# First batch rotated in tiles of later weights, its turns four slots apart, and weight conversion from slot -8 at 1.5 slots a block

## The chip, the cores and the metric

The kernel runs on one core of a Trainium2 chip. The metric is the device time of one execution in microseconds; the median over several runs is compared. TensorE multiplies, VectorE, ScalarE and GpSimd (POOL in the rows) do elementwise work, and SP issues the transfers.

## The reference, cut to what matters

Rotary attention for 4 batches of 8 heads, 576 positions and 64 columns, then two layers of two matrix products each, without a choice of experts: every token passes all of them.

```python
q_rot, k_rot = rotate(q), rotate(k)                    # (x1 c - x2 s, x1 s + x2 c), per position
scores = matmul(q_rot, k_rot.T) / sqrt(D)
attn = exp(scores - max); attn = attn / (sum(attn) + 1e-9)
x = (attn @ v) as 2304 tokens x 512
h = x @ w_in;  r = max(h, 0);  x = (s * r * r + b) @ w_out          # layer one, d_ff 2048
h = x @ w_in2; out = (h * sigmoid(1.702 h)) @ w_out2                # layer two
```

The weights arrive as 64-bit floats, the rest as 32-bit floats.

## The kernel before

**Stages.** Attention is cut into *slots*: one slot is one score tile of 128 query rows against 576 keys. A batch has 36 slots (four pairs of heads; first four tiles for each pair, then five for each), four batches have 144. Layer one and layer two follow in passes of 256 or 512 tokens; each pass walks the 16 *blocks* `f` of 128 hidden columns. Pass 0 of layer one needs 256 tokens of all heads, so its first matmul (tile `l`) can stand only some slots behind slot 15; from slot 22 on the kernel interleaves half steps of the passes with slots.

**Numbers in two parts.** Products are taken in two parts each (`hi`, `lo`), so a weight block is kept as four 128x512 pieces. `weight(layer, f, m)` makes half `m` of block `f`: `make_half` (L383) loads 512 KB of 64-bit words into a `stage` tile (L389 or L394), scales the high words on ScalarE (L398), joins the words to 32-bit floats on VectorE (a shift, L399, and two joins, L400 and L403), copies `hi` on ScalarE (L406) and subtracts on GpSimd (L407). Stage tiles come from the ring `xs` of four halves. Blocks in `HELD` stay in tiles `w0` to `w10`; the five others of layer one are spilled to DRAM (L430) and fetched again in each pass. `CONV = (-12, 1.0)` gives block `f` of layer one the slot -12 + f, so 0 to 15 fall in slots -12 to 3.

**Rotation.** For each batch, pair and side (key, query) `plan_rope` (L658) sets a load into tile `nat` (L186), two slots later two cross products into `rot` (L195), a product (L200) and a sum (L203), then two *turns* (L205): transposes on TensorE (L91), a copy on ScalarE (L216), a subtraction on VectorE (L217), both into `z`, and stores to DRAM (L223, L224). `nat` and `rot` have two buffers each, in the pool of attention. In batch 0 the pairs start at slots -16, -12, -8 and -4; the queries of pairs 0 and 1 (`RV = 2`) are rotated on VectorE, the six other tiles on GpSimd. The turns of pair p stand at slots -12 + 4p to -10 + 4p.

**A slot.** `fetch_pair` loads turned keys and queries again (L229, L239, L241) four slots ahead of a unit. `score_tile` (L281) multiplies (tile `s`), reduces on VectorE (L299) and takes the exponential on ScalarE (L308); `norm_tile` scales on GpSimd (L319); `turn_tile` transposes, and up to slot 19 (`SLO`) `rest_tile` forms the low part with TensorE and ScalarE. `weighted` multiplies by the values (tile `av`), and the result goes to DRAM as `xT` (L378), from where `prepare` (L479) loads it for a pass.

**Order.** `at(slot, fn, ...)` collects tasks, `ORDER` sorts those of one slot, and the loop at L779 issues them slot by slot with the slot as priority. The order of each engine's queue is fixed when the program is built, from these priorities and the builder's own costs; on the chip each queue runs in that order and waits for what it needs. A load waits on SP, in order, until its buffer is free.

Of the kernel before, what the change touches and what calls it, by code (L numbers as in the profile page):

```python
# [26 lines left out]
def kernel(  # L27
# [65 lines left out]
    def f32(ap):  # L93
        return ap.bitcast(F32)
# [28 lines left out]
    q_spill = dram.tile([B * NP, 128, 2 * S], F32, tag="qsp", name="qsp")  # L123
    v_spill = dram.tile([B * NP, 128, 4 * 5 * D], F16, tag="vsp", name="vsp")
    qd = {}
    kd = {}
# [44 lines left out]
    def v_spread(b, st):  # L171
# [9 lines left out]
        vsc[b] = sc  # L181

    def rope_load(b, p, which, st):
        nat = att.tile([128, RT, 2, HD], F32, tag="nat", name=f"nat{b}{p}{which}")
        src = (q, k)[which][b, 2 * p : 2 * p + 2]
        nc.sync.dma_start(  # L186
            nat.rearrange("a t e i -> a t (e i)"),
            src.rearrange("h (a t) d -> (h a) t d", t=RT),
        )
        st["nat"] = nat  # L190

    def rope_cross(b, p, which, st, eng):
        rot = att.tile([128, RT, 2, HD], F32, tag="rot", name=f"rot{b}{p}{which}")
        for e in range(2):
            eng.tensor_tensor(rot[:, :, e], st["nat"][:, :, 1 - e], tab[:, 2 - e], op=ALU.mult)  # L195
        st["rot"] = rot
# [186 lines left out]
    def make_half(t, w_in, w_out, f, m, nm):  # L383
        if late:
            raw = late["m2"].tile([128, 512], U64, tag="stage", name=f"stage{nm}{m}", bufs=3)
        else:
            raw = moe.tile([128, 512], U64, tag="xs", name=f"stage{nm}{m}", bufs=4)
        if m == 0:
            nc.sync.dma_start(  # L389
                raw.rearrange("p (c f) -> p c f", c=NCC),  # L390
                w_in[:, f * 128 : (f + 1) * 128].rearrange("(c p) f -> p c f", p=128),
            )
        else:
            nc.sync.dma_start(raw, w_out[f * 128 : (f + 1) * 128, :])  # L394
        words = raw.bitcast(U32).rearrange("p (n z) -> p n z", z=2)
        low, high = words[:, :, 0], words[:, :, 1]
        hi, lo = t[:, 0], t[:, 1]
        nc.scalar.activation(f32(high), f32(high), AF.Copy, scale=2.0**-112)  # L398
        nc.vector.tensor_scalar(low, low, 29, None, op0=ALU.logical_shift_right)  # L399
        nc.vector.scalar_tensor_tensor(  # L400
            low, high, 0x80000000, low, op0=ALU.bitwise_and, op1=ALU.bitwise_or
        )
        nc.vector.scalar_tensor_tensor(  # L403
            low, high, 3, low, op0=ALU.logical_shift_left, op1=ALU.bitwise_or
        )
        nc.scalar.copy(hi, f32(low))  # L406
        nc.gpsimd.tensor_tensor(lo, f32(low), f32(hi), op=ALU.subtract)  # L407

# [5 lines left out]
    def weight(layer, f, m):  # L414
# [8 lines left out]
        if f not in STREAMED[layer]:  # L423
            t = kept[layer][f][m]
        make_half(t, *W[layer], f, m, f"{layer}_{f}")
        if f in STREAMED[layer]:
# [31 lines left out]

    late = {}

    def x_tile(nm, z=0):
# [196 lines left out]
    def plan_rope(b, p, which, s, eng):  # L658
# [4 lines left out]
        at(s + 2, rope_add, b, p, which, st, eng)  # L663
        gap = 2 if b else 1
        for g in range(2):
            at(s + 4 + gap * g, rope_turn, b, p, which, g, st)

# [9 lines left out]
    R0 = 20  # L677
    CONV = (-12, 1.0)
    WPRI = 0
# [3 lines left out]
    SLO = 20  # L683
    RS, RL = 9, 16
    MOE_LATE = 500

# [6 lines left out]
    def target(s):  # L693
# [5 lines left out]
        return 0  # L699
    RV = 2  # L700
    slot = 0
# [31 lines left out]
    for b in range(B):  # L733
        plan_scales(b, bounds[b] - R0 if b else -LEAD + 1)
        for p in range(NP):
# [3 lines left out]
            for which in (1, 0):  # L739
                eng = nc.vector if b == 0 and p < RV and which == 0 else nc.gpsimd  # L740
                r = bounds[b - 1] + RS + 9 * p if b else -RL + 4 * p
                plan_rope(b, p, which, r + (1 - which), eng)
# [105 lines left out]
```

## Time and profile before

| what | us |
|---|---|
| median of 3 runs | 1307.54 (1304.89 to 1314.07) |
| the profiled execution | 1307.66 |
| its span | 1305.9 |
| TensorE busy with matmuls | 1119.6 (86%) |
| VectorE busy | 746.5 (57%) |
| ScalarE busy | 676.7 (52%) |
| GpSimd busy | 354.8 (27%) |

The shares are means over the whole span. In the page's 40 slices TensorE is busy less than 70% in each of the first six (up to 196 us) and 80% or more in all others but one; VectorE and GpSimd have most of their dense slices early. The engines must therefore be read by stretch.

### The profile page before, as it was taken

The page shows a single profiled execution, that of the slowest core. Times are in us where ns is not written, and L with a number is a line of the kernel's source. Part 1 is how long each engine was busy: PE and PEld are TensorE (multiplying, and loading weights), DVE is VectorE, ACT ScalarE, POOL GpSimd, SP SyncE. Part 2 cuts the span into 40 slices and gives each one's busy share as a digit, 9 for nine tenths or more (in the row PEclk, how much of TensorE's full clock was granted, in tenths as well). Part 3 has the DMA queues.
Part 4 walks back from the last instruction along what each step waited for, and adds up shares of the span by engine and source line. Part 5 has one row for each costly group of instructions (what it writes and reads, how often), then busy time and mean ns, then how long its engine had stood idle before and what let it go on. Part 6 is the DMA issues. An engine that isn't in the chain of part 4 may idle for free.

```text
span 1305.9 us, 21075 instructions
## 1 busy us (share of the span) xinstructions
PE 1119.6 (86%) x7432; PEld 991.4 (76%) x7432; DVE 746.5 (57%) x1652; ACT 676.7 (52%) x1483; POOL 354.8 (27%) x350
## 2 busy tenths in 40 slices
PE   0126568989989989999999996998999999999998
PEld 0024448988889888899889996876788888888887
DVE  7887735667657666757656657866633223232222
ACT  3347555666656666666656655665533223232232
POOL 5675743334324441444111112323100000000000
PEclk9998588999999999999999997999999999999999
DMA  7987765468756677665665528545303012021020
GB/s 241 307 272 243 243 173 149 139 196 252 224 155 211 197 230 228 191 212 169 187 195 172 166 73 289 166 148 170 117 17 113 1 49 81 17 74 24 17 81 17
DMA packets 131561, 202.50 MB, mean 155 GB/s; under 512 B 32512, under 2 KB 93440, under 8 KB 131456
## 3 DMA queue, kind: packets, MB, share of 16 engines
q1 hardware_dynamic: 131456, 201.15, 49.4%
q8 instruction: 59, 0.97, 0.3%
q14 instruction: 46, 0.38, 0.1%
HBM read 155.49 MB, written 45.61 MB: 154 GB/s over the span
## 4 chain that ended last, share of the span: by engine, by line
PE 56%; DMA 14%; DVE 9%; issue 8%; ACT 5%; POOL 4%; SPq 2%; DVEq 0%; POOLq 0%; ACTq 0%
PE acc L88 21%; PE l L88 21%; PE t L88 5%; PE s L88 4%; PE av L88 4%; DMA stage<-in_moe_w_in_dram 2%; DMA xT<-pt 2%; DVE P L299 2%; POOL w L407 2%; DMA xl<-xT 2%; DMA stage<-in_moe_w_out_dram 2%; DMA vr<-in_v_dram 1%; ACT P L308 1%; DVE stage L403 1%; DVE pt L342 1%
## 5 line engine op out<-in xcount | busy, mean ns | idle before, releaser
L88 PE MATMUL l<-xh,w 128*128 128x256 f32 (+1 forms) x1280 | 330.0, 331 | 11.9 <-ACT r L527 6.8
L88 PEld LDWEIGHTS l<-xh,w 128*128 128x128 f32 x1280 | 225.0, 191 | 36.0 <-ACT r L527 8.0
L88 PE MATMUL l<-xl,w 128*128 128x256 f32 (+1 forms) x640 | 211.8, 331 | 1.6 <-DVE xl L492 0.9
L319 POOL TENSOR_SCALAR P<-P,st 128x576 f32<-128x576 f32 x144 | 114.1, 793 | 345.3 <-DVE st L318 241.5
L88 PE MATMUL acc<-w,g 128*128 128x512 f32 x696 | 169.0, 392 | 4.9 <-ACT y L568 4.9
L308 ACT ACTIVATE P<-P,st 128x576 f32<-128x576 f32 x144 | 112.0, 778 | 101.8 <-DVE P L299 101.8
L532 DVE SCALAR_TENSOR_TENSOR r<-r,l 128x256 f32<-128x256 f32 x144 | 60.1, 417 | 180.2 <-ACT r L531 180.2
L88 PEld LDWEIGHTS acc<-w,g 128*128 128x128 f32 x696 | 131.1, 189 | 33.0 <-ACT y L568 5.8
L88 PE MATMUL t<-ident,P 128*128 128x128 f32 x720 | 111.7, 289 | 45.2 <-ACT pt L357 29.4
L531 ACT ACTIVATE r<-l 128x256 f32<-128x256 f32 x144 | 55.1, 383 | 178.9 <-PE l L88 178.8
L299 DVE TENSOR_SCALAR_CACHE_REDUCE P<-s 128x576 f32<-128x576 f32 x144 | 108.6, 754 | 62.9 <-PE s L88 57.4
L407 POOL TENSOR_TENSOR w<-stage,w 128x512 fp32r<-128x512 f32 x64 | 93.2, 1461 | 188.3 <-ACT w L406 146.2
L88 PEld LDWEIGHTS l<-xl,w 128*128 128x128 f32 x640 | 122.1, 191 | 13.3 <-DVE xl L492 2.0
L88 PEld LDWEIGHTS t<-ident,P 128*128 128x128 f32 x720 | 86.1, 148 | 58.7 <-issue 23.3
L88 PE MATMUL acc<-gh,w 128*128 128x256 f32 x616 | 129.4, 293 | 0.0
L88 PE MATMUL s<-k,qb 128*128 128x288 f32 x640 | 124.9, 324 | 3.9 <-DVE P L299 3.9
L342 DVE TENSOR_TENSOR pt<-t,pt 128x640 f16<-128x640 f32 x124 | 102.0, 822 | 28.3 <-ACT pt L340 27.6
L340 ACT CAST pt<-t 128x640 f16<-128x640 f32 x144 | 99.1, 688 | 21.2 <-PE t L88 19.4
L536 DVE TENSOR_TENSOR g<-r,g 128x256 fp32r<-128x256 f32 x160 | 71.0, 448 | 64.7 <-ACT g L535 64.7
L88 PEld LDWEIGHTS s<-k,qb 128*128 128x128 f32 x640 | 98.6, 204 | 12.2 <-issue 6.3
L529 ACT ACTIVATE r<-r,sb 128x256 f32<-128x256 f32 x144 | 86.1, 604 | 37.2 <-DVE r L528 36.7
L88 PEld LDWEIGHTS acc<-gh,w 128*128 128x128 f32 x616 | 102.6, 194 | 0.5 <-issue 0.4
(88 smaller groups left out, 1955.5 us busy)
## 6 DMA issues: line engine op xcount, KB each, us to landing
ws<-wd SPq DMA_DIRECT2D x96, 512.0 KB, 4.3
k<-ksp SPq DMA_DIRECT2D x32, 576.0 KB, 5.8
stage<-in_moe_w_in_dram SPq DMA_DIRECT2D x32, 512.0 KB, 5.0
stage<-in_moe_w_out_dram SPq DMA_DIRECT2D x32, 512.0 KB, 5.0
wd<-w SPq DMA_DIRECT2D x14, 512.0 KB, 5.0
ksp<-z SPq DMA_DIRECT2D x32, 160.0 KB, 5.0
qsp<-z SPq DMA_DIRECT2D x32, 160.0 KB, 4.4
vsp<-vz SPq DMA_DIRECT2D x16, 320.0 KB, 4.5
```

What stands on the lines that cost most here:

```text
L88: pin(nc.tensor.matmul(*args, **kw))
L299: nc.vector.tensor_scalar(pr.rearrange("p (n s) -> p n s", n=2), ps[:, :, :HS], -Q_SCALE, None, op0=ALU.mult, op1=ALU.min, accum_out=st[:, ...
L308: nc.scalar.activation(pr, pr, AF.Exp, bias=st[:, 0:1], scale=-1.0, accum_out=st[:, 1:2])
L319: nc.gpsimd.tensor_scalar(pr, pr, st[:, 2:3], 1.0, op0=ALU.mult, op1=ALU.mult)
L340: nc.scalar.copy(hi, pc)
L342: nc.vector.tensor_tensor(lo, pc, hi, op=ALU.subtract)
L403: nc.vector.scalar_tensor_tensor(low, high, 3, low, op0=ALU.logical_shift_left, op1=ALU.bitwise_or)
L407: nc.gpsimd.tensor_tensor(lo, f32(low), f32(hi), op=ALU.subtract)
L529: nc.scalar.activation(r, r, AF.Identity, bias=sb[:, 1:2], scale=sb[:, 0:1])
L531: nc.scalar.activation(r, ps[:, cols], AF.Tanh, scale=0.851)
L532: nc.vector.scalar_tensor_tensor(r, r, 1.0, ps[:, cols], op0=ALU.add, op1=ALU.mult)
L536: nc.vector.tensor_tensor(gl[:, cols], r, f32(gh[:, cols]), op=ALU.subtract)
```

## The change

Batch 0's rotation no longer uses `nat`. Each pair gets one tile with the tag of a later weight block, `w5` to `w8` (blocks 7, 9, 10 and 12): it holds query, key and the key's `rot`. All eight loads are issued at slots -16 to -12 (pair p at -16 + p), the rotations two slots behind, and the turns are set apart from them: key of pair p at -8 + 4p and -7 + 4p, query a slot later. `RV` is 3, so the queries of pairs 0 to 2 are rotated on VectorE, five tiles on GpSimd.

Conversion of layer one has `CONV = (-8, 1.5)`: block `f` at slot int(-8 + 1.5 f), 0 to 15 at slots -8 to 14. Blocks below 13 are staged in two tiles of the weights, `w10` for even and `w9` for odd blocks, each holding both halves of a block; blocks 13 to 15 use `xs` as before. In layer one the last two steps (copy of `hi`, subtraction) become a function `split` that is called a slot later (`WLAG`). `ACT_SHIFT` is empty, so the shift stays on VectorE.

```diff
--- before.py
+++ after.py
@@ -122,6 +122,8 @@
     k_spill = dram.tile([B * NP, 128, 2 * S], F32, tag="ksp", name="ksp")
     q_spill = dram.tile([B * NP, 128, 2 * S], F32, tag="qsp", name="qsp")
     v_spill = dram.tile([B * NP, 128, 4 * 5 * D], F16, tag="vsp", name="vsp")
+    boot = {}
+    BOOT = (5, 6, 7, 8)
     qd = {}
     kd = {}
     vsc = {}
@@ -180,8 +182,16 @@
         nc.vector.tensor_copy(inv[64:128, o : o + NP], pv[64:128, :, 1])
         vsc[b] = sc
 
+    def boot_part(p, i):
+        return boot[p][:, i * S : (i + 1) * S].rearrange("p (t e i) -> p t e i", t=RT, e=2)
+
     def rope_load(b, p, which, st):
-        nat = att.tile([128, RT, 2, HD], F32, tag="nat", name=f"nat{b}{p}{which}")
+        if b == 0:
+            if p not in boot:
+                boot[p] = wpool.tile([128, 2048], F32, tag=f"w{BOOT[p]}", name=f"boot{p}")
+            nat = boot_part(p, which)
+        else:
+            nat = att.tile([128, RT, 2, HD], F32, tag="nat", name=f"nat{b}{p}{which}")
         src = (q, k)[which][b, 2 * p : 2 * p + 2]
         nc.sync.dma_start(
             nat.rearrange("a t e i -> a t (e i)"),
@@ -190,7 +200,10 @@
         st["nat"] = nat
 
     def rope_cross(b, p, which, st, eng):
-        rot = att.tile([128, RT, 2, HD], F32, tag="rot", name=f"rot{b}{p}{which}")
+        if b == 0 and which == 1:
+            rot = boot_part(p, 2)
+        else:
+            rot = att.tile([128, RT, 2, HD], F32, tag="rot", name=f"rot{b}{p}{which}")
         for e in range(2):
             eng.tensor_tensor(rot[:, :, e], st["nat"][:, :, 1 - e], tab[:, 2 - e], op=ALU.mult)
         st["rot"] = rot
@@ -383,6 +396,12 @@
     def make_half(t, w_in, w_out, f, m, nm):
         if late:
             raw = late["m2"].tile([128, 512], U64, tag="stage", name=f"stage{nm}{m}", bufs=3)
+        elif f < HELD[0][-2]:
+            if m == 0:
+                stages[0] = wpool.tile(
+                    [128, 2, 512], U64, tag=f"w{len(HELD[0]) - 1 - f % 2}", name=f"stage{nm}"
+                )
+            raw = stages[0][:, m]
         else:
             raw = moe.tile([128, 512], U64, tag="xs", name=f"stage{nm}{m}", bufs=4)
         if m == 0:
@@ -396,15 +415,22 @@
         low, high = words[:, :, 0], words[:, :, 1]
         hi, lo = t[:, 0], t[:, 1]
         nc.scalar.activation(f32(high), f32(high), AF.Copy, scale=2.0**-112)
-        nc.vector.tensor_scalar(low, low, 29, None, op0=ALU.logical_shift_right)
+        if m in ACT_SHIFT and not late:
+            nc.scalar.activation(low, low, AF.Copy, scale=2.0**-29, bias=-0.5)
+        else:
+            nc.vector.tensor_scalar(low, low, 29, None, op0=ALU.logical_shift_right)
         nc.vector.scalar_tensor_tensor(
             low, high, 0x80000000, low, op0=ALU.bitwise_and, op1=ALU.bitwise_or
         )
         nc.vector.scalar_tensor_tensor(
             low, high, 3, low, op0=ALU.logical_shift_left, op1=ALU.bitwise_or
         )
-        nc.scalar.copy(hi, f32(low))
-        nc.gpsimd.tensor_tensor(lo, f32(low), f32(hi), op=ALU.subtract)
+
+        def split():
+            nc.scalar.copy(hi, f32(low))
+            nc.gpsimd.tensor_tensor(lo, f32(low), f32(hi), op=ALU.subtract)
+
+        return split
 
     W = ((w_in1, w_out1), (w_in2, w_out2))
     kept = ({}, {})
@@ -422,7 +448,11 @@
             kept[layer][f] = [t[:, 0:2], t[:, 2:4]]
         if f not in STREAMED[layer]:
             t = kept[layer][f][m]
-        make_half(t, *W[layer], f, m, f"{layer}_{f}")
+        split = make_half(t, *W[layer], f, m, f"{layer}_{f}")
+        if layer == 0:
+            at(int(CONV[0] + CONV[1] * f) + WLAG, split)
+        else:
+            split()
         if f in STREAMED[layer]:
             d = dram.tile([128, 2, 512], F32, tag=f"wd{layer}{f}{m}", name=f"wd{layer}{f}{m}")
             spill[layer][f, m] = d
@@ -457,6 +487,7 @@
             )
 
     late = {}
+    stages = {}
 
     def x_tile(nm, z=0):
         if late and z == 0:
@@ -661,9 +692,8 @@
         at(s + 2, rope_cross, b, p, which, st, eng)
         at(s + 2, rope_mul, b, p, which, st, eng)
         at(s + 2, rope_add, b, p, which, st, eng)
-        gap = 2 if b else 1
         for g in range(2):
-            at(s + 4 + gap * g, rope_turn, b, p, which, g, st)
+            at(s + 4 + 2 * g if b else 4 * p + RT0 - which + g, rope_turn, b, p, which, g, st)
 
     def plan_scales(b, s):
         st = {}
@@ -675,13 +705,16 @@
 
     LEAD = 12
     R0 = 20
-    CONV = (-12, 1.0)
+    CONV = (-8, 1.5)
     WPRI = 0
     LAG = 6
     SKEW_T = 2
     SPILL = 2
     SLO = 20
     RS, RL = 9, 16
+    RT0 = -7
+    ACT_SHIFT = ()
+    WLAG = 1
     MOE_LATE = 500
 
     def avail(n):
@@ -697,7 +730,7 @@
                 start = max(0, 2 * NF * n - SKEW)
                 return start + min(1.0, (s - lo) / (hi - lo)) * (2 * NF * (n + 1) - SKEW - start)
         return 0
-    RV = 2
+    RV = 3
     slot = 0
     starts = {}
     bounds = []
@@ -737,8 +770,8 @@
             for kk in range(2):
                 at(starts[b, p, kk] - 4, fetch_pair, b, p, kk)
             for which in (1, 0):
-                eng = nc.vector if b == 0 and p < RV and which == 0 else nc.gpsimd
-                r = bounds[b - 1] + RS + 9 * p if b else -RL + 4 * p
+                eng = nc.vector if b == 0 and (p < RV and which == 0) else nc.gpsimd
+                r = bounds[b - 1] + RS + 9 * p if b else -RL + p
                 plan_rope(b, p, which, r + (1 - which), eng)
             vt = {}
             at(first - 4, value_load, b, p, vt)
```

## Rows read from the trace of the kernel before

**Rows 1.** Timeline of TensorE, 190 to 196 us: start, length, instruction, wait.

```profile
194.63 0.58 PE L88 MATMUL l<-xh,w 128*128 128x256 f32 x1 [4.16 <-ACT xh L491]
```

**Rows 2.** Windows: length, then busy us (instructions) by engine, granted clock, DMA share, GB/s.

```profile
7.50:99.10 91.60, 18.73 (x66) 12.44 (x67) 82.24 (x113) 36.68 (x68) 64.40 (x50) 1.00 0.88 285
99.10:153.50 54.40, 32.04 (x172) 23.72 (x170) 46.19 (x83) 37.00 (x70) 38.49 (x31) 0.76 0.74 237
153.50:194.60 41.10, 26.20 (x173) 20.67 (x173) 14.60 (x52) 22.94 (x44) 16.60 (x21) 0.75 0.68 201
194.60:1305.90 1111.30, 1042.59 (x7022) 934.54 (x7022) 602.54 (x1399) 578.76 (x1302) 234.59 (x244) 0.98 0.45 139
```

**Rows 3.** Timeline of VectorE: score reductions of slots 0, 3, 14, 17, 21, 22.

```profile
70.93 0.76 DVE L299 TENSOR_SCALAR_CACHE_REDUCE P<-s 128x576 f32<-128x576 f32 x1 [0.40 <-PE s L88]
...
99.13 0.76 DVE L299 TENSOR_SCALAR_CACHE_REDUCE P<-s 128x576 f32<-128x576 f32 x1 [0.88 <-PE s L88]
...
158.79 0.76 DVE L299 TENSOR_SCALAR_CACHE_REDUCE P<-s 128x576 f32<-128x576 f32 x1 [2.16 <-PE s L88]
...
174.35 0.76 DVE L299 TENSOR_SCALAR_CACHE_REDUCE P<-s 128x576 f32<-128x576 f32 x1 [0.48 <-PE s L88]
...
187.27 0.76 DVE L299 TENSOR_SCALAR_CACHE_REDUCE P<-s 128x576 f32<-128x576 f32 x1 [0.37 <-PE s L88]
...
190.60 0.76 DVE L299 TENSOR_SCALAR_CACHE_REDUCE P<-s 128x576 f32<-128x576 f32 x1
```

**Rows 4.** Waits of TensorE, 0 to 200 us: total us, times, longest.

```profile
PE r L91 <- POOL nat L203: 47.2, 5, 12.9
```

**Rows 5.** Timeline, 7 to 21 us: rotation on GpSimd, conversion steps alone and colliding.

```profile
7.57 1.82 POOL L195 TENSOR_TENSOR rot<-nat,tab 128x288 f32<-128x288 f32 x2 [6.27 <-DMA nat<-in_k_dram]
...
9.47 1.50 POOL L200 TENSOR_TENSOR nat<-nat,tab 128x576 f32<-128x576 f32 x1
...
11.05 1.79 POOL L203 TENSOR_TENSOR nat<-nat,rot 128x576 f32<-128x576 f32 x1
...
13.72 0.68 DVE L400 SCALAR_TENSOR_TENSOR stage<-stage 128x512 uint32<-128x512 uint32 x1
14.32 0.41 DVE L399 TENSOR_SCALAR stage<-stage 128x512 uint32<-128x512 uint32 x1
...
18.73 1.30 POOL L407 TENSOR_TENSOR w<-stage,w 128x512 fp32r<-128x512 f32 x1 [1.33 <-ACT w L406]
18.81 1.76 DVE L400 SCALAR_TENSOR_TENSOR stage<-stage 128x512 uint32<-128x512 uint32 x1
```

**Rows 6.** Groups by line, VectorE then GpSimd, 0 to 153.5 us: busy, mean ns, idle.

```profile
L400 DVE SCALAR_TENSOR_TENSOR stage<-stage 128x512 uint32<-128x512 uint32 x32 | 34.3, 1071 | 5.7 <-ACT stage L398 4.9
...
L407 POOL TENSOR_TENSOR w<-stage,w 128x512 fp32r<-128x512 f32 x32 | 46.6, 1459 | 25.1 <-ACT w L406 24.9
...
L203 POOL TENSOR_TENSOR nat<-nat,rot 128x576 f32<-128x576 f32 x8 | 14.3, 1782 | 0.2
...
L319 POOL TENSOR_SCALAR P<-P,st 128x576 f32<-128x576 f32 x12 | 11.7, 976 | 16.1 <-DVE st L318 8.4 <-ACT stage L398 3.1 <-DMA vr<-in_v_dram 2.3
```

**Rows 7.** Timeline, 36 to 41 us: a query tile rotated on VectorE.

```profile
36.25 0.81 DVE L195 TENSOR_TENSOR rot<-nat,tab 128x288 f32<-128x288 f32 x2
...
37.59 0.75 DVE L200 TENSOR_TENSOR nat<-nat,tab 128x576 f32<-128x576 f32 x1
...
39.94 0.74 DVE L203 TENSOR_TENSOR nat<-nat,rot 128x576 f32<-128x576 f32 x1
```

**Rows 8.** Instructions on the stage tiles, 0 to 160 us: duration ns min/median/max, first and last.

```profile
L389 SPq DMA_DIRECT2D stage<-in_moe_w_in_dram x16: 378/433/740, 3.1 to 133.6; - x16
...
DMA to landing us min/median/max: 3.8/5.7/9.1
```

**Rows 9.** Waits of SP's queue, 0 to 200 us.

```profile
SPq L389 <- POOL w L407: 1.1, 2, 0.7
```

## The prediction, made before the changed kernel was timed

> **What bounds the kernel now.** The windows come first, because the busy shares of the whole span hide two regimes. From 194.6 us, where the first matmul of the experts stands [rows 1], to the end TensorE is busy 1042.59 of 1111.30 us, 94% [rows 2]. That stretch is TensorE's, and the change touches nothing in it. Before it, TensorE works 77 us of 194.6; these 194.6 us are what can be shortened.
>
> In that start, two stretches differ. Up to 153.5 us, VectorE is busy 82.24 of 91.6 us and then 46.19 of 54.4, GpSimd 64.40 and 38.49 [rows 2]. From 153.5 to 194.6 us the two have 14.60 and 16.60 us of work in 41.1. The first stretch holds the conversion of layer one's weights (32 halves) and the rotation; the second holds attention tiles alone, and its pace is set by the chain of one tile. So the start is two stretches laid end to end that could overlap: conversion with few tiles beside it, then tiles without conversion.
>
> The times of the score reductions (one for each slot) say the same [rows 3]: slot 0 at 70.93 us, slot 3 at 99.13, so 9.4 us a slot; from 3 to 14 5.4 us a slot; from slot 17 at 174.35 to slot 22 at 190.60 3.3 us. The waits of TensorE give the reason for the slow first slots: 47.2 us in five waits for the last addition of a rotation [rows 4]. The turns of pairs 2 and 3 stand ahead of slots 0 to 2 in TensorE's order, and the rotation of a pair can load only when one of two `nat` buffers comes free.
>
> What VectorE and GpSimd do to each other has to be priced before anything is moved. A shift alone takes 0.41 us, a join 0.68 (the second counted alike), the subtraction on GpSimd 1.30. But the join that starts at 18.81 us, 0.08 us after a subtraction, takes 1.76: it ends at 20.57, 0.54 us after the subtraction's end at 20.03 [rows 5]. So such operations run one after the other, not side by side; the mean join in the first stretch takes 1.07 us [rows 6]. The Trainium skill (SBUF — State Buffer, Who interferes with whom) says that a VectorE instruction with two SBUF inputs and a GpSimd instruction that reads SBUF hold a shared port for their whole length, the second waiting. The row agrees but for the tail.
>
> I therefore count the two engines' lone prices as one line of work. A half costs 0.41+0.68+0.68+1.30 = 3.07 us, and 32 halves 98.2 us. A rotated tile costs 1.82+1.50+1.79 = 5.11 us on GpSimd [rows 5] and 0.81+0.75+0.74 = 2.30 us on VectorE [rows 7]. Before 153.5 us GpSimd rotates eight tiles [rows 6]: six of batch 0 and two of batch 1, 40.9 us; VectorE rotates two, 4.6 us; twelve probabilities are scaled, 11.7 us. Together 155.4 us in the 146 us from 7.5: 1.064 us of lone work for each us. It is above one because tails overlap. This line is nearly full, and it bounds the first stretch.
>
> **The change, part by part.** *Rotation in the tiles of weights 5 to 8.* The eight loads go out in the first slots, none behind a buffer. No instruction is removed. The same 2.4 MB (eight tiles of 128x576 numbers of 4 bytes) move, earlier, past the first weight and value loads on SP; that delays the first conversion by six loads, and the rotation fills the line meanwhile, so I cost it at nothing. If the line stood idle instead it would cost the six loads, about 6 us at the 285 GB/s of that stretch [rows 2].
>
> *Turns four slots apart, from slot -7.* Only pairs 0 and 1 are turned ahead of slot 0. GpSimd's five tiles end no sooner than 7.6 + 5 x 5.11 = 33 us, and the turned tiles still go out to DRAM and back. So slot 0 lies between 33 and 70.93 us; I take 55, nearer the upper end, since the reload and the value scales remain. From there 17 slots at 5.4 us reach 147 us, earlier than the line of work below allows: the tiles' own chain does not decide.
>
> *One query tile more on VectorE* (`RV` 3): 5.11 - 2.30 = 2.8 us less on the line.
>
> *Conversion from slot -8 at 1.5 slots a block.* It removes no work. It lets tiles run beside conversion. By 55 us the line has cleared 47.5 x 1.064 = 50.5 us, of which eight rotated tiles are 5 x 5.11 + 3 x 2.30 = 32.5; so some three blocks are converted where the slots say five or six, and conversion trails its slots. It trails before too: block 15 belongs to slot 3 and its stage load leaves at 133.6 us [rows 8], ten slots on. I take it to end at slot 17 instead of its nominal 14.
>
> The sum for slot 17: conversion 98.2, seven tiles on GpSimd 35.8, three on VectorE 6.9, 17 scalings at 0.976 16.6, together 157.5 us. At 1.064 this ends at 7.5 + 148.0 = 155.5 us, against 174.35 before: 18.8 us won. Where tiles and conversion mix (99.1 to 153.5) VectorE is busy 85% of the time against 88% over both windows, so a rate of 1.03: 160.4 us, 13.9 won. I take 16. If conversion ended at slot 21 instead (two more rotated tiles, four more scalings, 171.6 us), the same rates win 18.5 and 13.2 against 187.27, so the lag matters little beyond slot 17. What follows is the old course: slot 22, the reload of xT, the first expert, and TensorE's 1111 us.
>
> Were the line strictly exclusive (a rate of 1.0), slot 17 would come at 165.0 us and 9.4 us would be won: 1298, which I count with the rival of no gain. That is the rule of the Trainium skill on the shared port (same page and section) taken by the letter; the 155.4 us of work done in 146 speak against the letter.
>
> *Late split and staging by whole blocks.* The split (copy and subtraction) falls a slot later, and the stage is two whole-block buffers in place of four half ones. No work is added; a block is held longer. I cost it at nothing while SP's stage loads do not wait; in the kernel before they waited 1.1 us for a subtraction [rows 9]. The price without that cover is the fourth rival.
>
> **The sum.** The profiled execution took 1307.66 us around its span of 1305.9; the median of the runs is 1307.54, so no correction. 1307.7 - 16 = 1291.7; I say 1291.
>
> **The rivals.**
> *Tiles leave conversion behind.* If conversion trails past slot 22, the line no longer holds the tiles; at 5.4 us a slot from 55 us slot 22 comes at 174, at the 3.3 of the last slots before at 128. The middle, 151, with 190.60 before, would win 40 us; but the later slots still queue behind some conversion, so I price it at 30 to 35: 1275. For it: conversion trails before by ten slots. Against it: late slots have less priority than due conversion.
> *Conversion keeps its slots, no gain worth naming.* It ends at slot 14: 154.6 us of work, at 152.8 or 157.6 us, against 158.79 [rows 3]: 1 to 6 us won, 1304. This is also the case in which the change does not do what it says, as the line of work was full before and stays so. For it: the 88%. Against it: the three blocks at 55 us.
> *SP held by whole-block staging: slower.* A block keeps its buffer for the landing, 5.7 us [rows 8], six VectorE steps at up to 1.07, a slot of 5.4, two subtractions at 1.46: 20.4 us. Two buffers then pass a block every 10.2 us; before, a block left every (133.6 - 3.1)/15 = 8.7. Each of 11 reuses could hold SP 20.4 - 17.4 = 3.0 us with the next unit's key and query loads behind it: 33 us. From 16 on it eats the gain; all of it gives 1325. Against it: fetches are issued four slots, over 20 us, ahead, and one hold is 3.
>
> **How the numbers follow.** Forecast (1283 to 1298) 0.45; tiles ahead 0.17; no gain (1298 to 1308) 0.23; SP held 0.15. The likeliest is 1291. The range 1272 to 1314 leaves out about half of the fastest case (0.08) and two thirds of the slowest (0.10). A measurement of this kernel can tell about 1%, 13 us, from no change: faster means under 1294.5, which is three quarters of the forecast and all of the first rival, 0.51; slower means over 1320.6, most of the last rival, 0.11; the rest, 0.38, is within 1%.
>
> **What would show it.** Right: slot 0's reduction at 50 to 60 us; TensorE's wait for rotations well under 20 us; last subtraction of the conversion at 155 to 170 us with slots 17 to 21 beside it; first expert matmul near 179 us; from there 1111 us as before. Wrong: slot 14 beside the last subtraction and the first expert after 189 (no gain); stage loads of SP waiting tens of us (slower); slot 22 before 160 (first rival). Also wrong if the stretch behind the first expert changes by over 5 us, for then the order of TensorE's work moved where I assumed it does not.

## The result, and the profile after

The changed kernel takes 1313.76 us (median of 22 runs, 1308.16 to 1319.67), the kernel before beside it 1306.82 (22 runs, 1292.06 to 1314.07). The ratio is 1.0058, 95% interval 1.0041 to 1.0075: slower by 0.6%, a small loss that the interval keeps clear of zero, where a gain of 1.3% was forecast. The profiled execution took 1316.7 us with a span of 1314.7; that of before 1307.66.

The two profiled executions differ by 9.0 us. The first expert matmul comes at 197.19 us, 2.6 later than before [rows 1]; from there to the end it is 1117.6 us, 6.3 more. These are the score reductions of slots 0, 3, 14, 17 and 22, on VectorE's timeline (start, length, instruction, wait), which answer [rows 3], and TensorE's first expert matmul:

```profile
67.59 0.76 DVE L312 TENSOR_SCALAR_CACHE_REDUCE P<-s 128x576 f32<-128x576 f32 x1 [0.41 <-PE s L88]
...
84.26 0.76 DVE L312 TENSOR_SCALAR_CACHE_REDUCE P<-s 128x576 f32<-128x576 f32 x1 [0.40 <-PE s L88]
...
156.63 0.75 DVE L312 TENSOR_SCALAR_CACHE_REDUCE P<-s 128x576 f32<-128x576 f32 x1
...
170.99 0.76 DVE L312 TENSOR_SCALAR_CACHE_REDUCE P<-s 128x576 f32<-128x576 f32 x1
...
188.40 0.76 DVE L312 TENSOR_SCALAR_CACHE_REDUCE P<-s 128x576 f32<-128x576 f32 x1
```

```profile
197.19 0.58 PE L88 MATMUL l<-xh,w 128*128 128x256 f32 x1 [8.91 <-ACT xh L522]
```

Slot 3 is 14.9 us earlier than before, slot 14 only 2.2, slot 17 3.4, slot 22 2.2; then the first expert matmul waits 8.91 us for its input, against 4.16, and the rest is lost. So the tiles do start earlier, beside the conversion, as meant; most of what they gain is gone by slot 14. The windows over the same stretches as [rows 2] show where (length, then busy us by engine in the order TensorE, its weight loads, VectorE, ScalarE, GpSimd, then granted clock, DMA share, GB/s):

```profile
7.50:99.10 91.60, 21.77 (x83) 15.31 (x83) 77.12 (x116) 34.74 (x64) 61.21 (x49) 0.94 0.72 230
99.10:153.50 54.40, 28.77 (x156) 21.07 (x157) 35.13 (x80) 36.98 (x70) 24.99 (x23) 0.59 0.86 273
153.50:194.60 41.10, 22.87 (x173) 17.96 (x171) 19.93 (x58) 24.21 (x46) 24.84 (x26) 0.87 0.83 273
194.60:1314.70 1120.10, 1049.23 (x7022) 939.68 (x7022) 601.31 (x1399) 579.06 (x1303) 235.57 (x244) 0.97 0.45 138
```

VectorE and GpSimd now leave room: in the second window they are busy 35.13 and 24.99 us of 54.4, against 46.19 and 38.49 before. TensorE's granted clock in that window is 0.59, against 0.76; with the later conversion alone, the kernel below that gains, it is 0.59 too, so it does not tell the loss from the gain. The room opens earlier still. The first window cut at 50 us, before and then after:

```profile
7.50:50.00 42.50, 6.73 (x22) 3.46 (x22) 39.04 (x57) 14.92 (x27) 24.97 (x21) 1.00 0.90 297
50.00:99.10 49.10, 12.00 (x44) 8.98 (x45) 43.20 (x57) 21.76 (x41) 39.42 (x30) 1.00 0.86 275
```

```profile
7.50:50.00 42.50, 2.65 (x9) 1.56 (x9) 40.90 (x40) 9.43 (x16) 37.84 (x27) 1.00 0.66 224
50.00:99.10 49.10, 19.11 (x74) 13.76 (x74) 36.22 (x78) 25.31 (x48) 23.36 (x22) 0.89 0.77 236
```

Up to 50 us GpSimd is busy 12.9 us more than before; from 50 to 99.1 it is busy 16.1 less, and DMA moves less in both. The two engines are crammed first and starved later. The transfers come late as well: up to 99.1 us some 5 MB less have been moved than before (rate times length of the windows), and from there to 194.6 us some 5 MB more, with the DMA engines busy 0.86 and 0.83 of the time, against 0.74 and 0.68. Between 20 and 153.5 us VectorE now stands for stage loads, 14.0 us in all; in the kernel before the same view has no such wait:

```profile
DVE stage L421 <- DMA stage<-in_moe_w_out_dram: 10.6, 6, 5.2
...
DVE stage L421 <- DMA stage<-in_moe_w_in_dram: 3.4, 4, 1.3
```

TensorE's waits up to 200 us name what it stood for in the meantime (total us, times, longest), beside [rows 4]:

```profile
PE r L91 <- DVE z L230: 28.9, 9, 8.8
PE r L91 <- POOL boot L216: 20.8, 1, 20.8
PE vps L88 <- DVE vm L149: 16.9, 1, 16.9
PE l L88 <- ACT xh L522: 8.9, 1, 8.9
```

The wait for rotations has fallen from 47.2 us in five to 20.8 in one, but that one is the first, 12.9 us before. The waits for `z`, VectorE's subtraction in a turn, have grown from 18.7 us to 28.9. And a new one stands there, 16.9 us for `vm`, the maxima of the values. On TensorE's timeline:

```profile
20.82 1.11 PE L91 MATMUL r<-ident,boot 128*128 128x128 f32 x4 [20.82 <-POOL boot L216]
...
52.79 0.58 PE L88 MATMUL vps<-ident,vm 128*1 128x128 f32 x2 [16.87 <-DVE vm L149]
53.74 0.42 PE L91 MATMUL r<-ident,boot 128*64 128x128 f32 x1 [0.37 <-DVE vrow L151]
```

The second turn of the first queries (53.74) stands behind `vps` in TensorE's order, so slot 0 hangs on the value maxima. Why these are late is on VectorE's timeline: the last two maxima stand between joins of blocks 13 and 14, which nobody needs yet.

```profile
49.37 0.68 DVE L425 SCALAR_TENSOR_TENSOR stage<-stage 128x512 uint32<-128x512 uint32 x1
49.98 0.74 DVE L141 TENSOR_REDUCE vmx<-vm 128x1 f32<-128x576 f32 x1
50.64 0.68 DVE L422 SCALAR_TENSOR_TENSOR stage<-stage 128x512 uint32<-128x512 uint32 x1
51.24 0.74 DVE L141 TENSOR_REDUCE vmx<-vm 128x1 f32<-128x576 f32 x1
```

The queue of SP shows how they came there. Blocks below 13 now have only two stage tiles, but blocks 13 and 14 go to `xs`, whose buffers nobody uses any more, and batch 1's first pair to `nat`, which batch 0 has left. All of them are issued in the first 18 us; block 2 follows only at 42.04 and 42.63. Two things stand ahead of it: the second subtraction of the conversion, which frees block 0's tile, ends at 38.7 us on GpSimd, and the stores of turned keys and queries, which wait for `z`, hold SP until 41.9:

```profile
11.88 0.61 SPq L196 DMA_DIRECT2D nat<-in_k_dram  x1
...
13.31 0.38 SPq L408 DMA_DIRECT2D stage<-in_moe_w_in_dram  x1
...
15.32 0.38 SPq L408 DMA_DIRECT2D stage<-in_moe_w_in_dram  x1
...
24.07 7.18 SPq L237 DMA_DIRECT2D ksp<-z  x2
31.50 3.78 SPq L236 DMA_DIRECT2D ksp<-z  x2
36.94 5.00 SPq L237 DMA_DIRECT2D qsp<-z  x2
...
42.63 0.44 SPq L408 DMA_DIRECT2D stage<-in_moe_w_in_dram  x1
```

GpSimd takes the key tiles of batch 0 not one after the other but in layers, the cross products of all four ahead of the sum of the first, and begins batch 1's rotation at 33 us, with three of batch 0's five sums still to come:

```profile
7.53 3.48 POOL L208 TENSOR_TENSOR boot<-boot,tab 128x288 f32<-128x288 f32 x4 [6.23 <-DMA boot<-in_k_dram]
10.97 3.18 POOL L213 TENSOR_TENSOR boot<-boot,tab 128x576 f32<-128x576 f32 x2
14.12 5.08 POOL L208 TENSOR_TENSOR boot<-boot,tab 128x288 f32<-128x288 f32 x4
19.16 3.18 POOL L216 TENSOR_TENSOR boot<-boot 128x576 f32<-128x576 f32 x2
...
33.03 2.17 POOL L208 TENSOR_TENSOR rot<-nat,tab 128x288 f32<-128x288 f32 x2
```

Nothing in the diff asks for that order. The old buffers enforced one: with two buffers of `nat` a tile could not be loaded before the last but one had left, and with four halves in `xs` block 13 not before block 11 had. With the buffers free, the builder put forward what was loadable.

### The profile page after: what moved, and what is told of

Read it like the earlier page. It is cut to its first block, busy times and chain, and to the rows that moved or that the text cites. A ratio compares the mean times of both kernels' runs of the same rounds, so it can differ in the third digit from the quotient of the medians.

```text
span 1314.7 us, 21007 instructions
## 1 busy us (share of the span) xinstructions
PE 1122.6 (85%) x7432; PEld 994.0 (76%) x7432; DVE 734.4 (56%) x1656; ACT 676.3 (51%) x1483; POOL 347.3 (26%) x346
## 4 chain that ended last, share of the span: by engine, by line
PE 55%; DMA 17%; DVE 10%; issue 6%; ACT 4%; SPq 3%; POOL 3%; DVEq 0%; POOLq 0%; ACTq 0%
PE l L88 21%; PE acc L88 21%; DMA stage<-in_moe_w_in_dram 4%; PE av L88 4%; PE t L88 4%; PE s L88 4%; DMA xT<-pt 2%; DMA stage<-in_moe_w_out_dram 2%; DVE P L312 2%; DMA xl<-xT 2%; DMA ksp<-z 2%; SPq L271 2%; DVE stage L422 2%; POOL w L431 1%; DVE pt L355 1%
## 5 line engine op out<-in xcount | busy, mean ns | idle before, releaser
L88 PE MATMUL l<-xh,w 128*128 128x256 f32 (+1 forms) x1280 | 333.6, 334 | 17.7 <-ACT xh L522 8.9
L88 PEld LDWEIGHTS s<-k,qb 128*128 128x128 f32 x640 | 97.5, 202 | 12.3 <-issue 6.9
L567 DVE TENSOR_TENSOR g<-r,g 128x256 fp32r<-128x256 f32 x160 | 70.9, 447 | 63.7 <-ACT g L566 63.7
```

Source lines behind the costliest of these rows:

```text
L88: pin(nc.tensor.matmul(*args, **kw))
L567: nc.vector.tensor_tensor(gl[:, cols], r, f32(gh[:, cols]), op=ALU.subtract)
```

## The experiments

The theory after this reading: the later conversion slots gain, and the rotation in the weights' tiles loses, through the order of work that it sets free. The rivals: whole-block staging holds SP (my fourth rival); the two engines' line was full and there was nothing to gain (my third); or what is lost lies only at the load of the first expert's input. `pin(ins, "name")`, a helper of the kernel, makes the builder issue the instructions of one name in the order in which the program writes them, without a semaphore of its own. The stations in us, each from the one profiled execution, then the median and the ratio to the kernel before that ran beside it (its medians went from 1306.3 to 1308.5 us, so rows are best compared by their ratios):

| kernel | slot 0 | slot 17 | last subtraction | first expert | from there on | median | ratio (95%) |
|---|---|---|---|---|---|---|---|
| before | 70.9 | 174.4 | 152.1 | 194.6 | 1111.2 | 1306.82 | |
| after | 67.6 | 171.0 | 168.3 | 197.2 | 1117.6 | 1313.76 | 1.0058 (1.0041 to 1.0075) |
| later conversion alone | 55.5 | 161.2 | 169.1 | 187.5 | 1115.2 | 1304.10 | 0.9967 (0.9941 to 0.9993) |
| rotation alone | 70.5 | 175.4 | 164.5 | 197.9 | 1116.1 | 1312.61 | 1.0046 (1.0021 to 1.0072) |
| after, half ring | 59.0 | 169.5 | 182.3 | 195.1 | 1114.0 | 1313.00 | 1.0039 (1.0013 to 1.0066) |
| after, block order | 60.5 | 169.5 | 182.5 | 198.9 | 1117.5 | 1318.16 | 1.0070 (1.0047 to 1.0093) |
| after, tile order | 66.3 | 175.8 | 169.8 | 199.0 | 1114.3 | 1315.95 | 1.0073 (1.0033 to 1.0112) |
| after, batch 1 held | 63.8 | 179.6 | 172.3 | 204.4 | 1116.7 | 1317.63 | 1.0076 (1.0053 to 1.0099) |
| after, all three orders | 53.4 | 167.9 | 165.7 | 189.2 | 1116.4 | 1305.13 | 0.9985 (0.9960 to 1.0010) |
| after, block and tile order | 57.0 | 169.3 | 167.4 | 195.9 | 1120.0 | 1311.16 | 1.0042 (1.0021 to 1.0064) |
| all three orders, half ring | 53.5 | 165.6 | 170.6 | 190.6 | 1111.3 | 1307.49 | 0.9997 (0.9971 to 1.0022) |
| later conversion, input first | 56.4 | 159.8 | 168.1 | 181.4 | 1114.2 | 1300.92 | 0.9962 (0.9946 to 0.9978) |
| all three orders, input first | 53.5 | 168.9 | 166.1 | 191.4 | 1113.6 | 1304.78 | 0.9975 (0.9942 to 1.0009) |
| before, input first | 71.0 | 172.4 | 151.7 | 192.9 | 1117.8 | 1308.89 | 0.9994 (0.9964 to 1.0024) |

**The two halves of the change, each alone.** The kernel before with the conversion's slots alone:

```diff
-    CONV = (-12, 1.0)
+    CONV = (-8, 1.5)
```

> The kernel before with one edit: conversion of layer one from slot -8 at 1.5 slots a block; rotation through two buffers, staging in the ring and the immediate split stay. Theory D (the later slots of conversion alone lose, since conversion waits where the two engines were free): the last subtraction at 160 to 175 us, slot 17 no earlier than 174, 1308 to 1314. Rival E (the later slots are what helps the tiles): slot 17 at 165 to 170 us and 1300 to 1305.

It gains 0.33%. The first turn stays at 12.87 us, `vps` comes at 40.24 and slot 0's scores at 54.14, 12 us earlier than in the changed kernel. TensorE's timeline:

```profile
12.87 1.11 PE L91 MATMUL r<-ident,nat 128*128 128x128 f32 x4 [12.87 <-POOL nat L203]
...
40.24 0.59 PE L88 MATMUL vps<-ident,vm 128*1 128x128 f32 x2 [1.45 <-DVE z L217]
...
54.14 1.30 PE L88 MATMUL s<-k,qb 128*128 128x288 f32 x4
```

Slot 17 is 13 us earlier than before, the first expert matmul 7, the median 4.4. That is rival E, with slot 17 still earlier than it asked.

The other half: rotation in the weights' tiles, the old conversion and staging. Since `w10` and `w9` hold no stages here, the pairs take tiles `w7` to `w10`; the turns stand where they stood for the conversion of before:

```diff
+    BOOT = (7, 8, 9, 10)
...
+            nat = boot_part(p, which)
...
-    RV = 2
+    RV = 3
+    RT0 = -11
+    WLAG = 0
...
-                r = bounds[b - 1] + RS + 9 * p if b else -RL + 4 * p
+                r = bounds[b - 1] + RS + 9 * p if b else -RL + p
```

> The kernel before with the rotation alone: the eight tiles of batch 0 loaded at once into the tiles of later weights (blocks 10, 12, 13 and 15 here, so that conversion in its old slots finds them free in time), three query tiles on VectorE, turns in their old slots, conversion as before in the ring. Theory F (rotating all tiles at once delays the first pair, whose sum then comes at 20 us instead of 12.8, and gains only for pairs 2 and 3): slot 0 at 66 to 72 us, slot 3 at 85 to 92 instead of 99, 1302 to 1307. Rival G (the rotation is what costs): slot 0 after 73 us and 1310 or more.

It loses 0.46% alone, with `RV` 3 in it: rival G by the time, though slot 0 (70.5 us) came as theory F had it. The first turn waits as long as in the changed kernel, with no new staging and no new conversion slots (TensorE's waits); and the conversion, in its old slots, ends 12.3 us later than before, at 164.5:

```profile
PE r L91 <- POOL boot L216: 21.0, 1, 21.0
```

So the two halves are told apart: one gains, the other loses, and staging by blocks is not needed for the loss. The two add up to 0.13%, and the change has 0.58%; that the halves also hurt each other is likely, but the intervals, added at their edges, overlap. Where they meet is `xs`, tested next.

**Staging: half ring.** The changed kernel without the two whole-block tiles; all blocks in `xs` again:

```diff
-        elif f < HELD[0][-2]:
-            if m == 0:
-                stages[0] = wpool.tile(...)
-            raw = stages[0][:, m]
```

> The changed kernel with its staging undone: every half is staged in the ring of four half buffers as before; rotation, slots and the late split stay. Theory B (two whole-block buffers pace the conversion, 8.7 us a block, with VectorE and GpSimd half idle): a block comes every 6 to 7.5 us, the last subtraction at 140 to 155 us, and the first expert at 188 to 193, 1306 to 1310. Rival C (what paces it is the slot that conversion is given, or the transfers): the last subtraction stays at 165 to 175 us and the time within 3 us of the changed kernel's.

Slot 0 comes at 59.0 us in place of 67.6, since blocks 13 and 14 can't jump ahead, but the last subtraction at 182.3 in place of 168.3, later than either theory had it. The ratio's interval overlaps that of the changed kernel: no difference that can be told.

**Order of blocks.** The stage loads pinned in block order:

```diff
+        if not late:
+            pin(ins, "stage")
```

> The changed kernel with one edit: the stage loads of layer one are issued in the order of the blocks, so that blocks 13 and 14, staged in the free ring, no longer go ahead of block 2. Theory A (their early loads and joins hold up the value maxima, and so the turn of the first queries and slot 0): the value maxima end before 40 us instead of 52, slot 0's reduction comes at 55 to 60 us instead of 67.6, and the first expert matmul is 3 us or more earlier, 1308 to 1311. Rival B (conversion is paced by its two whole-block buffers, and the two early blocks were its only lead): slot 0 moves up but the last subtraction of the conversion comes at 175 to 185 us instead of 169.6, and the time stays at 1313 to 1320.

Slot 0 at 60.5 us, so blocks 13 and 14 ahead of the values were worth 7 us there. The conversion now ends at 182.5, and at the first expert matmul nothing is left of the 7 us.

**Order of tiles.** The rotation of batch 0 pinned tile by tile on each engine:

```diff
+    def chained(b, eng, ins):
+        if b == 0:
+            pin(ins, "rope_v" if eng is nc.vector else "rope_g")
...
```

> The changed kernel with one edit: batch 0's rotated tiles are finished one after the other on each engine (cross products, product and sum of a tile before the next tile's). Theory A (the tiles are worked through in layers, so the first pair's sum comes at 20.8 us instead of 12.9 and everything up to slot 0 is late by that): the first turn at 12 to 14 us, slot 0 at 57 to 62 us instead of 67.6, 1308 to 1312. Rival B (the first pair's time is not what holds slot 0; the value maxima behind blocks 13 and 14 are): the first turn early all the same, slot 0 within 3 us of 67.6 and the time within 3 us of the changed kernel's.

The first turn comes at 12.3 us again, yet the value maxima stay at 50 us and slot 0 at 66.3: the first turn alone is not the path.

**Batch 1 held.** The first pair's loads of batch 1 pinned behind the first store of `xT`:

```diff
+        if b == 1 and p == 0:
+            pin(ins, "nat")
...
+        if b == 0 and p == 0 and q0 == 0:
+            pin(ins, "nat")
```

> The changed kernel with one edit: the loads of batch 1's first pair are kept behind the first result of batch 0. In the changed kernel they leave at 11.9 us, because the two buffers that batch 0 no longer uses are free, and its rotation takes some 10 us of GpSimd before slot 0. Theory A (this early work of batch 1 is a good part of what keeps slot 0 late): slot 0 3 to 8 us earlier than 67.6, the first expert 2 to 5 us earlier. Rival B (GpSimd's work is only moved, and TensorE waits for VectorE there): slot 0 within 2 us and the time within 3 us of the changed kernel's.

Slot 0 comes 3.8 us earlier, but slot 17 8.6 later: the two tiles are now rotated between 144 and 164 us, in the middle of the last conversions.

**All three together.** None of the three helps the time alone. If they are links of one path, they must be mended together:

```diff
+            pin(ins, "rope_v" if eng is nc.vector else "rope_g")
...
+        if b == 1 and p == 0:
+            pin(ins, "nat")
...
+        if not late:
+            pin(ins, "stage")
```

> The changed kernel with three edits together: stage loads in block order, rotated tiles finished one after the other, batch 1's first loads kept behind the first result. Theory A (the rotation costs only through these three orders): slot 0 at 45 to 52 us, slot 17 at 155 to 163, the first expert at 180 to 190, 1295 to 1305, no slower than the kernel with conversion's later slots alone (1304). Rival B (conversion is held by its two whole-block buffers whatever leads): slot 0 early, but the last subtraction still after 165 us, slots 17 to 22 stretched, the first expert at 193 to 199 and 1310 to 1318.

Slot 0 comes at 53.4 us, the first expert matmul at 189.2, the median is 1305.13. That is 8.6 us under the changed kernel, with intervals that don't meet. The order of the work is thus shown as the cause of the loss against the kernel before: the edit changes the order of the builder's queues, and no size, buffer or operation. It is not shown as the cause of all that is missing from the forecast. Slot 0 lies just outside theory A and slot 17 (167.9 us) 5 us outside; the last subtraction, at 165.7, is where rival B had it. DMA moves 201 GB/s from 7.5 to 50 us, where the kernel before had 297, and VectorE still stands for stage loads between 20 and 153.5 us:

```profile
DVE stage L431 <- DMA stage<-in_moe_w_in_dram: 11.2, 6, 5.3
```

Whether these late transfers hold the conversion is open: no run takes the stores that wait for `z` out of the way of the stage loads on SP. The pairs of orders other than the next one were not tried either.

Two of the three, with batch 1 free:

```diff
+            pin(ins, "rope_v" if eng is nc.vector else "rope_g")
...
+        if not late:
+            pin(ins, "stage")
```

> The changed kernel with two orders written out: the rotation of batch 0 tile by tile on each engine, and the conversion's stage loads in block order; the rotation of batch 1's first pair stays free to go early. Three orders together gave slot 0 at 53.4 us and 1305.1 us. Theory A (the path of the first pair and of the values alone decides, batch 1's two tiles fill room that was idle): slot 0 at 53 to 56 us, first expert matmul at 188 to 192, 1303 to 1308 us. Rival B (the 10 us that two tiles of batch 1 take on GpSimd before slot 0 count in full, since GpSimd and VectorE work as one line): slot 0 at 60 to 65 us, first expert matmul at 195 or later, 1311 to 1317 us.

Slot 0 comes at 57.0 us, between the two expectations; the first expert matmul at 195.9 and 1311 us are what rival B, the line of work, says. The interval lies above that of the three orders. GpSimd's timelines show the one difference, batch 1's first tiles at 38 to 67 us in the first, from 132 in the second:

```profile
37.64 2.06 POOL L212 TENSOR_TENSOR rot<-nat,tab 128x288 f32<-128x288 f32 x2
...
55.12 1.41 POOL L220 TENSOR_TENSOR nat<-nat,rot 128x576 f32<-128x576 f32 x1
```

```profile
132.53 1.55 POOL L214 TENSOR_TENSOR rot<-nat,tab 128x288 f32<-128x288 f32 x2 [1.99 <-DMA nat<-in_k_dram]
```

Work put forward early should come back as room later. It doesn't: at slot 17 the two kernels are 1.4 us apart, and at slot 20 8.2 (186.5 and 178.3). Why the room stays unused isn't settled.

The three orders with the half ring:

```diff
-                stages[0] = wpool.tile(...)
...
+            pin(ins, "stage")
```

> The changed kernel with the three orders put right (e11) and with every half staged in the ring of four half buffers as before. Theory A (what is left of the loss is that a block keeps a whole buffer): the last subtraction before 160 us instead of 165.7, slots 12 to 17 earlier by 3 us or more, 1300 to 1303 instead of 1305. Rival B (staging is no limit; conversion trails because tiles go first): the last subtraction at 163 to 180 us and the time within 2 us of 1305.

1307.49 beside 1305.13, with overlapping intervals. Under the mended order too the staging makes no difference that can be told.

**The load of the first input.** In the changed kernel the store of the last unit that pass 0 needs stands behind nine value loads of batch 1 on SP, and the reload `xl` behind it:

```profile
179.51 6.75 SPq L271 DMA_DIRECT2D vr<-in_v_dram  x9
...
186.99 0.38 SPq L391 DMA_DIRECT2D xT<-pt  x1
...
190.13 0.38 SPq L521 DMA_DIRECT2D xl<-xT  x1
```

Pinned ahead of the value loads, in three kernels: in the one with the later conversion alone, in the one with three orders, and in the kernel before. The edit:

```diff
-                if first:
+                if first or (b == 1 and p < 2):
                     pin(ins, "V")
...
+        if b == 0 and p == 3 and q0 == 0:
+            pin(ins, "V")
...
+            if n == 0:
+                pin(ins, "V")
```

> The kernel before with conversion's later slots, and the store of the last quarter of pass 0's tokens and their reload put ahead of the value loads of batch 1 on SP. Theory A (the end of the start is the store, the reload and what stands ahead of them on SP): the store leaves at most 1 us after its data are there, the first expert comes 8 us or less behind it, 183 to 186 us instead of 187.5, and 1300 to 1303. Rival B (the first expert is not what binds by then): the first expert earlier, the time unchanged at 1304.

> The changed kernel with the three orders put right (e11), and the store and reload of pass 0's last quarter ahead of batch 1's value loads on SP as in e9. Theory A (two independent losses): the first expert at 182 to 186 us instead of 189.2, 1300 to 1303. Rival B (in this kernel the store already leaves early enough): first expert at 188 to 190 and 1304 to 1306.

> The kernel before with the store and reload of pass 0's last quarter ahead of batch 1's value loads on SP, nothing else. Theory A (the store waits on SP for 1 us there and the reload lands among value loads): the first expert 2 to 4 us earlier than 194.6, 1303 to 1306. Rival B: no change within 2 us of 1307.

With the later conversion the first expert matmul comes at 181.4 us, the earliest of all; SP now stores, reloads and only then loads the values:

```profile
171.72 0.38 SPq L378 DMA_DIRECT2D xT<-pt  x1
...
174.49 0.38 SPq L492 DMA_DIRECT2D xl<-xT  x1
174.91 7.29 SPq L258 DMA_DIRECT2D vr<-in_v_dram  x10
```

The median is 1300.92, below both kernels (0.9962 to before, interval 0.9946 to 0.9978). Against the later conversion without it, the median is 3.2 us lower, but the two ratios (0.9962 and 0.9967) can't be told apart. With the three orders the first expert matmul came at 191.4 us, outside both expectations and 2.2 later than without the edit; in the kernel before it came 1.7 earlier. In these two kernels the order of these loads makes no difference that can be measured: 1304.78 beside 1305.13, and 1308.89 beside 1307.80. By the times the value loads on SP are a small matter. The edit was not made in the changed kernel itself, where the first expert matmul waits longest (8.91 us).

## Why the prediction failed, step by step

**The two engines as one line of work: held with the old rotation.** The sum of prices said that slot 17 comes at 155.5 to 160.4 us; with conversion in slots -8 to 14 alone, another kernel but nearly the same sum of work, it came at 161.2. There the line did its work at the mixed rate that I had taken, 1.03: by 170.4 us it had done 32 halves (98.2), nine tiles on GpSimd (46.0), two on VectorE (4.6) and 19 scalings (18.5), 167.3 us of work at my prices in 162.9, a rate of 1.027. The Trainium skill (SBUF — State Buffer, Who interferes with whom) states that the second of two such instructions blocks for the whole of the first. By that the rate could not pass 1.0. My rates don't decide this, for my GpSimd prices were not lone ones: VectorE rotated a query tile in the same microseconds as [rows 5], and 0.976 was the mean scaling. The shortest in the trace of the kernel before are 0.79 us for a cross product, 1.40 for a product, 1.41 for a sum and 0.74 for a scaling, so a tile is 4.4 us and the rate before about 1.0 (my sum: 146.8 us of work in 146.0). The forecast hardly moves, since prices and rate fall together, but a line at a rate of 1.0 then has slot 17 at 155.9 us and not at the 165.0 of the prediction. Against the strict rule stand other rows, of the changed kernel: while GpSimd does four cross products in 5.08 us from 14.12 us on (shown above), VectorE does, among others,

```profile
15.95 2.60 DVE L216 TENSOR_TENSOR boot<-boot,rot 128x576 f32<-128x576 f32 x2
```

That is one instruction of each every 1.3 us, where the lone 0.79 and 0.75 add up to 1.54.

**The rate in the changed kernel: the step that failed.** By slot 17 (171.0 us) it had done 32 halves, seven tiles on GpSimd (35.8), three on VectorE (6.9) and 16 scalings (15.6), 156.5 us in 163.5, a rate of 0.957. At 1.03 the same work takes 151.9 us: the line did 11.6 us less than I had it do, and most of the gain of 16 that I had forecast for slot 17 went there; 3.4 were left. I had named a price, "if the line stood idle instead", of about 6 us for the six loads. I set it at nothing because "the rotation fills the line meanwhile". It did fill the line, until 50 us; the idle came after, when TensorE's turns and SP's stage loads were late. The conversion's first subtraction starts at 29.93 us in place of 16.11. With the three orders put right the same 156.5 us of work are done by 167.9 us, a rate of 0.976: the orders are a part of the idle line, and what the rest of it is stays open (the late transfers above are the rival that no run tests).

**"No instruction is removed", "none behind a buffer": right, and the reason for the loss.** I looked at which loads are moved past which, not at what the two buffers of `nat` and the four of `xs` had been keeping in order. Freed, they took in batch 1's first pair and blocks 13 and 14, and the rotation was issued in layers. The three orders put right give slot 0 at 53.4, where I had 55, and get 8.6 us back.

**Turns and slot 0.** I took 55 between 33 and 70.93: it is 67.6 in the changed kernel. 55 holds for the later conversion alone (55.5) and for the three orders (53.4).

**Conversion trails its slots.** Right in the changed kernel: the last subtraction comes at 168.3 us, behind slot 15, where I had slot 17 and 155 to 170 us. In the other kernels with the later slots it comes at 165.7 to 182.5 us, beside slots 15 to 19.

**"What follows is the old course": failed in part.** From slot 17 to slot 22 it took 16.2 us before, and to the first expert matmul 20.3. In the changed kernel it took 17.4 and 26.2: all of the 3.4 us won at slot 17 and 2.6 more are lost there, most of it in the longer wait for the input. With the later conversion alone it took 22.7 and 26.3, for the last conversions and a rotation of batch 1 now lie beside these slots. So of 13.2 us won at slot 17 only 7.1 reach the first expert. With the input's load put first they took 17.4 and 21.6, and the expert came at 181.4, near my 179.

**"The change touches nothing in it", TensorE's 1111 us: mis-sized.** 1117.6 in the changed kernel and 1113.6 to 1120.0 in eleven of the twelve others; one has 1111.3. I had named a change of over 5 us there as a sign that the order of TensorE's work had moved. It had not: from about 170 us on TensorE's instructions stand in the same order in both traces. What differs is the granted clock, below, and by these profiles it differs as much without the change.

**Late split and staging by whole blocks.** The half ring makes no measurable difference, with and without the three orders, as I had it; the late split was not tried apart. The rival of SP held by whole blocks (1325) named a queue that was indeed held, but by stores waiting for `z`, not by stage loads waiting for a buffer.

**The rivals, and the range.** 1313.76 lies inside the range (1272 to 1314) by a quarter of a microsecond, and only because the range took in part of the slowest rival: that is no merit of the forecast. It lies above the 1298 to 1308 of no gain (1304) and below SP held (1325), and neither has the mechanism: no gain had conversion keep its slots and the line stay full. Conversion trailed, and the line was not full. Tiles leaving the conversion behind (1275) is excluded by slot 22 at 188.4.

`RV` 3 was not tried apart from the rotation; its 2.8 us can't be seen.

## What to carry to other kernels

A buffer is also an order: before a load is given a buffer of its own, list what the old buffer kept back, and expect the builder to put all of it forward, ahead of what the first result needs. Count a line of work only as full as its queues allow; a forecast of overlap needs the order of each queue, the value maxima's and the store's too, not only the sum of prices. Where three orders are wrong at once, mending any one may show nothing; test them together before the theory is dropped.

## What the runs showed of the hardware

The stretch behind the first expert matmul is TensorE's, and in these traces its time moves with the granted clock. Slots 36 to 108 took 344.0 us before and 352.7 after, with the clock at its lower level for 0.2 us of it before and 20.5 after (summed over the clock records of the two traces). One such place, TensorE's timeline and the window from 375 to 380 us, before:

```profile
370.94 0.39 PE L88 MATMUL l<-xh,w 128*128 128x256 f32 x1 [2.78 <-ACT r L527]
```

```profile
375.00:380.00 5.00, 5.00 (x44) 5.00 (x43) 3.83 (x12) 3.58 (x8) 1.00 (x2) 1.00 0.04 8
```

and after:

```profile
372.73 0.58 PE L88 MATMUL l<-xh,w 128*128 128x256 f32 x1 [3.60 <-ACT r L558]
```

```profile
375.00:380.00 5.00, 5.00 (x28) 4.24 (x27) 2.25 (x11) 2.66 (x6) 0.75 (x1) 0.63 0.00 2
```

A wait of 3.60 us stands before the fall, one of 2.78 where the clock stayed at 1.00; the same 5 us then hold 28 matmuls in place of 44, all busy. From the first expert matmul to the end the lower level (1.2 GHz in place of 2.4) holds for 42.9 us before and 56.0 after; 13.1 us more at half speed cost up to 6.6. The same 7022 matmuls keep TensorE busy for 1042.59 us before [rows 2] and 1049.23 after (the last of the windows above): 6.6 us more, which covers the 6.3 that were lost.

That the change brings this about is not shown. The kernel before with the input first has TensorE's whole order unchanged and nothing of the change, and its profiled execution took 1117.8 us in this stretch, with 56.2 us at the lower level and TensorE busy for 1049.44. Its ten executions took from 1299.57 us, at a mean granted clock of 0.969, to 1312.45, at 0.955, and the profiled one is the slowest. So one profile of each kernel can't put these 6.3 us down to the change. Nor does the clock account for every kernel: with the later conversion alone the stretch is 3.9 us longer than before at 43.4 us of low clock, and what else is longer there stays open.
